# A delta-rule attention and soft-MoE kernel: block inverse, a wider join product, output products by batch row

## The chip, the cores and the metric

The kernel runs on one core of one Trainium2 chip. The metric is the device time of one execution in microseconds. A core has a matrix engine (TensorE, PE in the profile; PEld is its loading of weights), a vector engine (DVE), a scalar engine (ACT), a general engine (POOL) and a queue engine that issues transfers (SP). All data is fp32; the profile shows each fp32 matrix product as two instructions with a weight load each, and each transpose as one.

## The reference

```python
def _attn_ref(q, k, v, beta):                    # (4, 8, 768, 48)
    k_n = k / (np.linalg.norm(k, axis=-1, keepdims=True) + 1e-06)
    state = np.zeros((B, H, D, D))
    for t in range(S):
        y[:, :, t] = np.einsum('bhd,bhde->bhe', q[:, :, t], state)
        v_old = np.einsum('bhde,bhd->bhe', state, kt)
        state = state + bt * np.einsum('bhd,bhe->bhde', kt, vt - v_old)

def _moe_ref(x, phi, w1, w2):                    # x (3072, 384), phi (384, 32)
    logits = x @ phi                             # w1 (8, 384, 1024), w2 (8, 1024, 384)
    d = softmax(logits, axis=0); slot_input = (d.T @ x).reshape(8, 4, 384)
    for e in range(8):
        slot_out[e] = np.maximum(slot_input[e] @ w1[e], 0.0) @ w2[e]
    c = softmax(logits, axis=1)
    return c @ slot_out.reshape(32, 384)
```

The softmaxes are written out here in one word each. The attention output, with batch and time as rows and head and feature as columns, is x.

## The kernel before

The 768 time steps are cut into 12 chunks of 64, and the sequential update inside a chunk is replaced by a triangular system per head. There are 32 heads in all (4 batches of 8); a pair of heads shares the 128 partitions, and pairs are numbered j = 0 to 7, with i for one of two head groups and c for the half of the partitions.

For each chunk `prep` (line 653) loads k and q, turns them with eight 128x128 transposes each (`turn`, line 563), forms the Gram products k k and k q (`gram`, line 589), and copies the key part out of PSUM under row masks (`keys`, line 620, two ACT instructions per half: two of the three 32-column blocks at once, then the third). `pack` (line 675) adds the two 32-blocks on the diagonal of each head's 64x64 matrix for the inversion.

`invert` works on two chunks together. The matrices are spread (line 727) so that each partition holds two 16x16 blocks, and each block is inverted by columns on DVE: `scale` (line 767) multiplies all 16x16 entries by the weights, then `col(j)` for j = 0 to 14 makes a product (line 777) and a subtraction (line 781) over the rows below j. The results are turned back (lines 799 and 807) and copied into the layouts of the joins (`wide`, line 818).

`join` builds the 64x64 inverse from the 16x16 ones in two steps. From 16 to 32: the copies `far16`, the products `m16` (line 854: 16 per chunk, with weights of 128 rows and 64 columns, one head each, and 32 moving columns), copies `ev16` (line 862), the products `mo16` (line 872), and the correction at line 878. From 32 to 64: line 884 turns, line 895 copies, `mq` (906), `mo64` (917) and the correction at line 927.

`step(n)` then applies the chunk to the state: state times keys (959), the rest (966), the inverse times the rest (979), the copy of that result (1003), the update of the state (1017, 1026), and the output of the chunk from the state (989) and from inside the chunk (1041, copied at 1052). `route` turns the output (1077) and forms the logits (1102); `phase` keeps the running softmax over rows (1162 to 1191) with the slot products (1180).

The last stage starts when all chunks are through: line 1279 gathers the slot inputs, `first` multiplies with w1 (1304) and turns the hidden layer (1320), `combine` makes the softmax over slots (transposes 1120 and 1135, six each, and the DVE and ACT work at 1124 to 1137), `second` multiplies with w2 (1339) in two column halves of 192, line 1350 adds the expert parts, and line 1361 forms the output: for each stretch of 256 rows and each batch b two products with 32 rows of the combine weights against the 32 slots. DVE or ACT copies the result (1363), and SP sends it out (1365).

The order of all this is not the order of the program text. Every operation is recorded with an engine, a planned duration, the buffers it reads and writes and a key. A list scheduler (`Plan.schedule`) then plays the engines forward, picks per engine the ready operation with the longest remaining path plus its key, finds it room in SBUF (52,900 columns) and PSUM (eight banks), and the instructions are issued in that order, each engine in its own queue. Keys are shifted by the table `SHIFT`, one number for each kind of operation. The planner also models the supply of PE instructions in blocks (`FETCH`, `BESIDE`) and fills idle PE time in two stretches with products whose result is not used (line 480). Weight transfers start after chunk 6 (w1) and 10 (w2) and as soon as room is left (`WKEEP`, `W2KEEP`).

The lines that carry the change:

```python
            for j, i in pairs:                                       # m16, 16 products
                x = xi(i, j)
                mm(A(p16)[ha(i), 0, 32 * j:32 * j + 32], A(Gk[n])[:, 96 * x:96 * x + C],
                   A(z16)[:, 32 * x:32 * x + 32])
```

Of the kernel before, what the change touches and what calls it, by code (L numbers as in the profile page):

```python
# [16 lines left out]
SLACK = 4.53  # L17
HEAD = 40.0
SHIFT = {
# [45 lines left out]
class Tensor:  # L65
# [4 lines left out]
    BLOCK, AHEAD, FETCH, BESIDE = 256, 64, 3.8, 5.0  # L70
# [264 lines left out]
def kernel(  # L335
# [17 lines left out]
    nc = tc.nc  # L353
# [42 lines left out]
    def t_act(c):  # L396
        return 0.17 + 0.00071 * c
# [88 lines left out]
    W1AT, W2AT, W2KEEP = 6, 10, 8741  # L486
# [35 lines left out]
    for s_ in H2:  # L522
        for u in H2:
            def pick(s_=s_, u=u):
                for y in H2:
                    o = A(bsel)[0:32, P * (2 * s_ + u):P * (2 * s_ + u) + P].rearrange(
                        "p (c u s y i j) -> p u s y c i j", c=2, u=2, s=2, y=2, i=2)[:, u, s_, y]
                    x = ident()[0:32, 0:32].rearrange("p (y j i c) -> p y c i j", y=2, i=2, c=2)[:, y]
# [28 lines left out]
    def turn(src, n, w):  # L557
# [17 lines left out]
        pl.op("DVE" if dve else "ACT", t_dvp(1024) if dve else t_act(1024), ev, r=[ps], w=[(KQ[n], w)],  # L575
# [24 lines left out]
    def G3(n):  # L600
        return A(Gk[n]).rearrange("p (x b t) -> p x b t", b=3, t=32)

    def keys(n, j0, nj, ps, w):

        def ev(ys, i, lower):
            def go():
                i_ = A(ps).rearrange("p i (y j f) -> p i y j f", j=4, f=w)[..., 0:C].rearrange(
                    "p i y j (b t) -> p i y j b t", b=2)
                o = G3(n).rearrange("p (y i j) b t -> p i y j b t", y=2, i=2)
                i_, o, m = (i_[..., 1, :], o[..., 1, :], M1()) if lower else (i_, o[..., 0::2, :], M0())  # L610
                if i is None:
                    i_, o = i_[:, :, ys[0] - j0 // 4], o[:, :, ys[0]]
                elif len(ys) == 2:
                    i_, o = i_[:, i], o[:, i]
                else:
                    i_, o = i_[:, i, ys[0]], o[:, i, ys[0]]
                if i:
                    nc.vector.tensor_scalar(o, i_, m, None, op0=ALU.mult)
                else:
                    nc.scalar.activation(o, i_, ACT.Copy, scale=m)  # L620
            c = 512 if i is None and not lower else 256
            pl.op("DVE" if i else "ACT", t_dvp(c) if i else 0.61 if c == 512 else t_act(c), go, r=[(ps, i), cm0],
                  w=[(Gk[n], (lower, y, i)) for y in ys])
        for i in H2 if n == 1 else (None,):
            for y in range(j0 // 4, (j0 + nj) // 4):
                ev((y,), i, 0)
                if i is None:
                    ev((y,), i, 1)
            if i is not None:
                ev(H2, i, 1)  # L630
# [3 lines left out]
    def queries(n, j0, nj, ps, w):  # L634
# [8 lines left out]
        if j0 + nj == 8:  # L643
            qt = pl.buf(512)
            pl.op("ACT", 0.50, lambda: nc.scalar.activation(  # L645
# [9 lines left out]
    def prep(n):  # L655
# [16 lines left out]
        def pack():  # L672
            x = G3(n).rearrange("p x b t -> p b x t")
            o = A(Gd[n // 2]).rearrange("p (t s x) -> p s x t", s=2, t=32)[:, n % 2]
            (nc.vector if n == 1 else nc.gpsimd).tensor_tensor(o, x[:, 0], x[:, 1], op=ALU.add)  # L675
# [29 lines left out]
    def invert(gs):  # L705
        G = len(gs)
        head = gs[0] == 0
        if head:
            for n in H2:
                squares(n)  # L710
            for y, c in ((0, 0), (0, 1), (1, 0), (1, 1)):
                def turn_sq(y=y, c=c):
                    o = A(sqh)[ha(c ^ y)].rearrange("p (s y i j) -> p s y j i", s=2, y=2, i=2)[:, :, y]
                    x = A(sqn)[ha(c)].rearrange("p (s y j i) -> p s y j i", s=2, y=2, i=2)[:, :, y]
# [47 lines left out]

        def scale():
            for a in range(G):
                o = blk(lb, 0, 16, 0, 16)[:, 2 * a:2 * a + 2]
                m = A(gm)[:, 32 * a:32 * a + 32].rearrange("p (x t) -> p x t", x=2)
                V.tensor_tensor(o, o, m.unsqueeze(2).broadcast_to([P, 2, 16, 16]), op=ALU.mult)
        pl.op("DVE", (t_dv(512) + 0.08) * G, scale, r=[gm], w=[lb], port=True)
        pr = pl.buf(2 * G * 64)

        def col(j):
            m, w = j + 1, 15 - j

            def go():
                p = A(pr)[:, 0:2 * G * m * w].rearrange("p (x i k) -> p x i k", x=2 * G, k=m)
                sh = [P, 2 * G, w, m]
                V.tensor_tensor(p, blk(tt, j, j + 1, 0, m).broadcast_to(sh),  # L777
# [12 lines left out]
        for j in range(15):  # L790
            col(j)
# [606 lines left out]
```

## Time and profile before

| | us |
|---|---|
| median of 3 runs (lowest, highest) | 285.26 (282.96, 285.4) |
| the profiled execution, and its span | 285.92, 283.9 |
| PE products of line 589 / 563 / 1041 / 989 | 26.3 / 25.6 / 18.6 / 18.7 |
| PE unused products (line 480) | 23.6 |
| ACT copies of line 620 (47) | 25.6 |
| POOL `pack`, line 675 (11) | 14.2 |
| w1 and w2 transfers issued on SP | 164.0 to 259.8 |
| output transfers issued on SP | 262.8 to 280.9 |

The profile is of one execution. Busy times of engines overlap, so they do not add up to the span. The chain of waits is one path back from the last instruction: at each step to what released it, or to the instruction before it on the same engine. An engine's share of that chain says more about the end than its busy time.

### The profile page before, as it was taken

The page shows a single profiled execution, that of the slowest core. Times are in us where ns is not written, and L with a number is a line of the kernel's source. Part 1 is how long each engine was busy: PE and PEld are TensorE (multiplying, and loading weights), DVE is VectorE, ACT ScalarE, POOL GpSimd, SP SyncE. Part 2 cuts the span into 40 slices and gives each one's busy share as a digit, 9 for nine tenths or more (in the row PEclk, how much of TensorE's full clock was granted, in tenths as well). Part 3 has the DMA queues.
Part 4 walks back from the last instruction along what each step waited for, and adds up shares of the span by engine and source line. Part 5 has one row for each costly group of instructions (what it writes and reads, how often), then busy time and mean ns, then how long its engine had stood idle before and what let it go on. Part 6 is the DMA issues. An engine that isn't in the chain of part 4 may idle for free.

```text
span 283.9 us, 13766 instructions
## 1 busy us (share of the span) xinstructions
PE 253.4 (89%) x6038; PEld 211.2 (74%) x6038; DVE 203.6 (72%) x445; ACT 164.7 (58%) x350; POOL 99.0 (35%) x212
## 2 busy tenths in 40 slices
PE   8999998999987989797998998869997999999970
PEld 4777688898876978696986997768886896367860
DVE  2789988989688696789888796869971646941340
ACT  5556498678654698566778479671673452240330
POOL 8933476527730087404474027610330100000000
PEclk9999999999999999999999999989999999999995
DMA  8999982929436390066580994596997889999966
GB/s 99 142 137 145 137 90 41 135 43 139 59 50 68 68 106 3 2 82 93 99 75 2 125 236 97 163 228 218 330 373 265 246 249 322 328 301 329 289 216 223
DMA packets 105834, 45.11 MB, mean 159 GB/s; under 512 B 77008, under 2 KB 99568, under 8 KB 105776
## 3 DMA queue, kind: packets, MB, share of 16 engines
q1 hardware_dynamic: 105600, 44.05, 74.3%
q8 instruction: 47, 0.77, 1.2%
q10 hardware_dynamic: 48, 0.10, 0.3%
q0 software_dynamic: 128, 0.10, 0.2%
q14 instruction: 11, 0.09, 0.1%
HBM read 39.52 MB, written 4.72 MB: 156 GB/s over the span
## 4 chain that ended last, share of the span: by engine, by line
PE 65%; ACT 9%; DMA 7%; issue 6%; DVE 5%; SPq 3%; POOL 1%; ACTq 0%; DVEq 0%; POOLq 0%
DMA sb<-in_k_dram 7%; PE pb L589 6%; PE pb L563 6%; PE pb L989 5%; PE pb L959 5%; PE pb L979 5%; PE pb L480 4%; PE pb L872 4%; PE pb L1339 4%; PE pb L1304 4%; PE pb L1017 4%; PE pb L1041 4%; PE pb L854 3%; PE pb L917 2%; PE pb L1102 2%
## 5 line engine op out<-in xcount | busy, mean ns | idle before, releaser
L574 ACT ACTIVATE sb<-pb 128x1024 f32<-128x1024 f32 x23 | 23.5, 1025 | 17.5 <-PE pb L563 17.4
L620 ACT ACTIVATE sb<-pb,sb 128x256 f32<-128x256 f32 (+1 forms) x47 | 25.6, 574 | 7.1 <-PE pb L589 5.3
L777 DVE TENSOR_TENSOR sb<-sb 128x30 f32<-128x30 f32 (+7 forms) x90 | 27.0, 300 | 2.7
L589 PE MATMUL pb<-sb 48*64 48x64 f32 (+1 forms) x1024 | 26.3, 247 | 2.4 <-ACT sb L574 1.1
L589 PEld LDWEIGHTS pb<-sb 48*64 48x64 f32 x1024 | 22.3, 134 | 6.1 <-ACT sb L574 2.2
L563 PE MATMUL pb<-sb 128*128 128x128 f32 x192 | 25.6, 277 | 1.1 <-DMA sb<-in_k_dram 1.1
L781 DVE TENSOR_TENSOR sb<-sb 128x30 f32<-128x30 f32 (+7 forms) x90 | 23.7, 264 | 3.1
L675 POOL TENSOR_TENSOR sb<-sb 128x512 f32<-128x512 f32 x11 | 14.2, 1289 | 32.8 <-ACT sb L620 28.5
L480 PE MATMUL pb<-sb 128*128 128x512 f32 (+3 forms) x72 | 23.6, 456 | 1.1 <-DVE sb L449 1.1
L563 PEld LDWEIGHTS pb<-sb 128*128 128x128 f32 x192 | 20.9, 141 | 3.0 <-issue 1.4
L895 POOL COPY sb<-sb 32x128 f32<-32x128 f32 x48 | 13.7, 285 | 26.6 <-DVE sb L878 21.7
L1003 ACT COPY sb<-pb 64x768 f32<-64x768 f32 (+1 forms) x24 | 18.4, 765 | 6.1 <-PE pb L979 5.7
L1026 DVE TENSOR_TENSOR sb<-sb,pb 48x768 f32<-48x768 f32 x20 | 19.0, 952 | 3.7 <-PE pb L1017 3.3
L480 PEld LDWEIGHTS pb<-sb 128*128 128x128 f32 x72 | 13.0, 201 | 10.0 <-issue 7.8
L649 POOL TENSOR_SCALAR_AFFINE_SELECT sb<-sb 64x512 f32<-64x512 f32 x24 | 16.2, 676 | 11.1 <-ACT sb L645 6.9
L1041 PE MATMUL pb<-sb 128*64 128x96 f32 x384 | 18.6, 248 | 1.5 <-issue 1.5
L989 PE MATMUL pb<-sb 128*64 128x96 f32 x352 | 18.7, 260 | 0.0
L895 ACT COPY sb<-sb 32x128 f32<-32x128 f32 x48 | 14.2, 295 | 7.3 <-DVE sb L878 5.0
L1052 ACT ACTIVATE sb<-pb 128x768 f32<-128x768 f32 x11 | 8.9, 811 | 16.3 <-PE pb L1041 16.2
L1041 PEld LDWEIGHTS pb<-sb 128*64 128x64 f32 x384 | 16.6, 137 | 2.2 <-issue 1.9
L1017 PE MATMUL pb<-sb 128*48 128x96 f32 x352 | 16.9, 248 | 1.4 <-ACT sb L645 0.7
L884 DVE STREAM_TRANSPOSE sb<-sb 64x512 f32<-64x512 f32 x24 | 16.9, 705 | 0.6
(157 smaller groups left out, 544.9 us busy)
## 6 DMA issues: line engine op xcount, KB each, us to landing
sb<-in_moe_w_dram SPq DMA_DIRECT2D x48, 256.0 KB, 4.7
sb<-in_moe_w_dram SPq DMA_DIRECT2D x32, 384.0 KB, 6.6
sb<-in_k_dram SPq DMA_DIRECT2D x24, 192.0 KB, 5.5
sb<-in_v_dram SPq DMA_DIRECT2D x48, 96.0 KB, 4.4
sb<-in_q_dram SPq DMA_DIRECT2D x24, 192.0 KB, 6.1
out_dram<-sb SPq DMA_DIRECT2D x24, 192.0 KB, 2.5
sb<-in_beta_dram ACTq DMA_DIRECT2D x1, 96.0 KB, 4.9
sb<-in_moe_phi_dram POOLq DMA_DIRECT2D x2, 32.0 KB, 6.0
```

The costliest lines, as they stand in the source:

```text
L480: pl.filler = lambda b, w: mm(A(b)[:, 0, 0:w].rearrange("p (a f) -> p a f", f=min(w, P)), A(cone), A(cone)[:, 0:min(w, P)].unsqueeze(1).br ...
L563: nc.tensor.transpose(o[:, 128 * j:128 * j + 128], A(src)[:, 128 * j:128 * j + 128], ident())
L574: nc.scalar.activation(o, x, ACT.Copy)
L589: mm(A(ps)[ha(c ^ (j // 4)), i, w * (j - j0):w * (j - j0) + w], kq(n)[hd(i), j, c, 0:C], kq(n)[hd(i), j, c, lo:hi])
L620: nc.scalar.activation(o, i_, ACT.Copy, scale=m)
L777: V.tensor_tensor(p, blk(tt, j, j + 1, 0, m).broadcast_to(sh), blk(lb, j, j + 1, j + 1, 16).rearrange("p x a i -> p x i a").broadcast_to(s ...
L781: V.tensor_tensor(t, t, p, op=ALU.subtract)
L895: (nc.scalar.copy if by_act else nc.gpsimd.tensor_copy)(o[q:q + 32, :, c, i], zx()[64 * c + 32:64 * c + 64, y, i].rearrange("p (j t) -> p ...
L989: mm(ypart(j)[:, :, c], kq(n)[:, j, c, C:2 * C], S0()[:, j, c], start=b % 2 == 0 and c == 0)
L1017: mm(A(pS)[hd(i), j // 4, a:a + 2 * D], A(Kb[n])[:, 128 * j + 64 * i:128 * j + 64 * i + D], U0()[:, j // 4, i, j % 4])
L1026: nc.vector.tensor_tensor(o, o, x, op=ALU.add)
L1041: mm(ypart(j)[:, i], A(AT[n])[:, C * xi(i, j):C * xi(i, j) + C], U0()[:, j // 4, i, j % 4], start=n == 0 and b % 2 == 0 and i == 0)
```

## The change

Five things change, and a new order comes out of them.

1. `invert`: columns are only worked off inside the two 8x8 diagonal blocks of each 16x16 block (7 pairs instead of 15, on four blocks of 8 per partition), `scale` multiplies only those, and the 8x8 block below the diagonal is then formed by two products and two reductions. The POOL copy `place` goes; its place in the layout is taken by a different order of heads in the buffers, so that several access patterns change with it.

```diff
-        for j in range(15):
+        for j in range(7):
             col(j)
+        pl.op("DVE", 1.3, upper, r=[lb, tt], w=[pr], port=True)
+        pl.op("DVE", 1.15, lambda: V.tensor_reduce(
+            A(low), A(pr).rearrange("p (x j) -> p x j", j=8), axis=AX.X, op=ALU.add), r=[pr], w=[low])
+        pl.op("DVE", 1.3, lower, r=[low, tt], w=[pr], port=True)
+        pl.op("DVE", 1.3, below, r=[pr], w=[tt])
```

`upper` and `lower` each issue two DVE products of 512 elements per partition, `below` two reductions of 512 to 64.

2. `m16`: one product for both heads of a pair. The weights are 128 columns wide, the moving operand 64 columns; half of the result is not used.

```diff
-            for j, i in pairs:
-                x = xi(i, j)
-                mm(A(p16)[ha(i), 0, 32 * j:32 * j + 32], A(Gk[n])[:, 96 * x:96 * x + C],
-                   A(z16)[:, 32 * x:32 * x + 32])
-        o16 = pl.op("PE", **t_pe(16, 0.059, 32.0), fn=m16, r=[Gk[n], z16], w=[p16])
+            for j in range(8):
+                mm(A(p16)[:, 0, C * j:C * j + C], A(Gk[n])[:, 192 * j:192 * j + P], A(z16)[:, C * j:C * j + C])
+        o16 = pl.op("PE", **t_pe(8, 0.118, 64.0), fn=m16, r=[Gk[n], z16], w=[p16])
```

3. `keys`: the key blocks lie as (pair, head and block) instead of (head, block), and each of the three blocks is copied by an instruction of its own. For chunks 4 to 11 that is six copies of 256 elements instead of two of 512 and two of 256; for chunks 0, 2 and 3 three of 512.

4. The output products of the four batches are one operation, and the batches take turns; each batch has a PSUM bank of its own.

```diff
+                for par in H2:
+                    for b in range(B):
+                        rg = slice(32 * b, 32 * b + 32)
+                        mm(A(po[b])[:, 0, HD * par:HD * par + HD], A(cT)[rg, T0 + par:T0 + 256:2], A(so)[rg])
```

5. The plan: `combine` may start after the last chunk's product instead of after line 1279 (`combine(g, [chain[N - 1]])`); planned durations of ACT copies (`t_act`) go from 0.17 + 0.00071 c to 0.23 + 0.0007 c; `FETCH` 3.8 to 4.1 and `BESIDE` 5.0 to 6.0; `SLACK` 4.53 to 5.77; `W2KEEP` 8741 to 1000, `WKEEP` 4836 to 8236; and all of `SHIFT` is new. In the order that results, the w1 transfers come as 14 and 34 around the last v load instead of 6, 6 and 36 around the last two; the softmax transposes lie before and among the w1 products instead of just before and after them; and the output products of the first half take turns with the w2 products of the second.

More of the change, by code (lines that the diff above doesn't have):

```diff
@@ L574, in ev @@
                 nc.scalar.activation(o, x, ACT.Copy)
[L575 removed]
+        pl.op("DVE" if dve else "ACT", t_dvp(1024) if dve else 0.91, ev, r=[ps], w=[(KQ[n], w)],
               key=-30 if dve else 0)
@@ L617, in go @@
[L617 to L623, printed above, removed]
-        for i in H2 if n == 1 else (None,):
[L625 to L630, printed above, removed]
+                x = A(ps).rearrange("p i (j f) -> p j i f", f=w)[:, :, :, 32 * (b > 0):32 * (b > 0) + 32]
@@ new lines, in go @@
+                o, m = Gb(n, b)[:, j0:j0 + nj], M1() if b == 1 else M0()
+                if i is not None:
+                    o, x = o[:, :, i], x[:, :, i]
+                if i:
+                    nc.vector.tensor_scalar(o, x, m, None, op0=ALU.mult)
+                else:
+                    nc.scalar.activation(o, x, ACT.Copy, scale=m)
+            c = 32 * nj * (2 if i is None else 1)
+            pl.op("DVE" if i else "ACT", t_dvp(c) if i else t_act(c) + 0.03, go, r=[(ps, i), cm0], w=[(Gk[n], (b, j0, i))])
@@ L632 @@
+        for i in H2 if n == 1 else (None,):
+            for b in (0, 1, 2):
+                ev(i, b)
     APART = 4
@@ L761, in invert @@
         pl.op("DVE", W_, lambda: V.tensor_copy(dg(tt), sv(gm)), r=[gm], w=[tt])
+        d8 = lambda t, r0, r1, c0, c1: bass.AP(
+            tensor=A(t).tensor, offset=A(t).offset, ap=[list(A(t).ap[0]), [264, 4], [1, 264]])[
+            :, :, 0:256].rearrange("p x (r c) -> p x r c", c=32)[:, :, r0:r1, c0:c1]
         def scale():
[L764 to L767, printed above, removed]
@@ new lines, in invert, with upper, lower @@
+        lo8 = lambda x: A(low)[:, 64 * x:64 * x + 64].rearrange("p (i k) -> p i k", k=8)
+        sh8 = [P, 8, 8, 8]
+        def upper():
+            for x in H2:
+                V.tensor_tensor(p8(x), blk(lb, 0, 8, 8, 16)[:, x].rearrange("p j i -> p i j").unsqueeze(2).broadcast_to(sh8),
+                                blk(tt, 0, 8, 0, 8)[:, x].rearrange("p j k -> p k j").unsqueeze(1).broadcast_to(sh8), op=ALU.mult)
+        def lower():
+            for x in H2:
+                V.tensor_tensor(p8(x), blk(tt, 8, 16, 8, 16)[:, x].unsqueeze(2).broadcast_to(sh8),
+                                lo8(x).rearrange("p i k -> p k i").unsqueeze(1).broadcast_to(sh8), op=ALU.mult)
@@ new lines, in below @@
+        def below():
+            for x in H2:
+                V.tensor_reduce(blk(tt, 8, 16, 0, 8)[:, x], p8(x), axis=AX.X, op=ALU.add, negate=True)
+        pl.op("DVE", 0.14, lambda: V.transpose(A(nT), A(nrm)), r=[nrm], w=[nT])
+        for j in range(7):
+            col(j)
+        pl.op("DVE", 1.3, upper, r=[lb, tt], w=[pr], port=True)
+        pl.op("DVE", 1.15, lambda: V.tensor_reduce(
+            A(low), A(pr).rearrange("p (x j) -> p x j", j=8), axis=AX.X, op=ALU.add), r=[pr], w=[low])
@@ L1327 @@
     for g in range(NG):
-        combine(g, [ot3])
+        combine(g, [chain[N - 1]])
     for hc in H2:
```

112 lines of the change are left out of this document (49 added, 63 removed), and 45 rows, old and new, of the table SHIFT.

## The prediction

> **What bounds the kernel now.** I read the page's engine row first, then the chain of waits, then busy time by stretch, and last the groups that the change touches.
>
> ```profile
> PE 253.4 (89%) x6038; PEld 211.2 (74%) x6038; DVE 203.6 (72%) x445; ACT 164.7 (58%) x350; POOL 99.0 (35%) x212
> ...
> PE 65%; ACT 9%; DMA 7%; issue 6%; DVE 5%; SPq 3%; POOL 1%; ACTq 0%; DVEq 0%; POOLq 0%
> ```
>
> TensorE is busy nearly all the time and holds 65% of the chain. DVE is busy 72% but holds 5%: its work mostly lies beside TensorE's. "issue" is mostly TensorE stopping inside a product with nothing to wait for (at 72.7, 78.0, 87.1, 114.6, 170.8, 185.8, 212.9 and 216.8 us, 0.8 to 2.1 each). The page counts 47 instruction packets of 16 KB; in the trace they never start less than 4.04 us apart, so dense stretches of small products run out of instructions.
>
> ```profile
> 75.00:100.00 25.00, 22.75 (x632) 20.30 (x632) 19.28 (x48) 15.42 (x27) 5.18 (x18) 1.00 0.47 64
> 145.00:175.00 30.00, 27.49 (x776) 24.71 (x775) 23.79 (x54) 21.88 (x41) 10.01 (x24) 1.00 0.61 111
> 200.00:225.00 25.00, 21.87 (x662) 19.98 (x662) 15.82 (x21) 14.92 (x31) 5.91 (x14) 1.00 0.87 296
> ```
>
> The columns are length, then busy time of PE, PEld, DVE, ACT, POOL. In every stretch of the chunk loop PE is filled to 87 to 92%, so a product that gets longer can hide only in the rest. The groups concerned, then the weight loads of line 537 and the products of line 854 in time:
>
> ```profile
> L854 PE MATMUL pb<-sb 128*64 128x32 f32 x384 | 13.4, 223 | 0.0
> L1361 PE MATMUL pb<-sb 32*128 32x192 f32 x96 | 9.1, 342 | 0.5 <-DVE sb L1351 0.5
> L777 DVE TENSOR_TENSOR sb<-sb 128x30 f32<-128x30 f32 (+7 forms) x90 | 27.0, 300 | 2.7
> L781 DVE TENSOR_TENSOR sb<-sb 128x30 f32<-128x30 f32 (+7 forms) x90 | 23.7, 264 | 3.1
> ...
> 11.33 0.97 PEld L537 LDWEIGHTS pb<-sb 128*128 128x128 f32 x8
> ...
> 111.72 1.13 PE L854 MATMUL pb<-sb 128*64 128x32 f32 x32
> ```
>
> An fp32 product shows as two pieces. L854 is the first join product: 32 pieces whose weights are 64 columns wide, two column tiles side by side, in 1.05 to 1.13 us. L537 is the nearest row to what replaces it: weights 128 columns wide, 32 moving columns, eight pieces whose loads start 0.111 us apart.
>
> **First join product.** 32 pieces become 16 with 128-column weights and 64 moving columns. In L854 a pair of pieces starts every 0.058 us: 16 x 0.058 = 0.93. By L537's spacing the new one takes 16 x 0.111 = 1.78. So +0.85 us per chunk, 12 chunks, +10.2 us of TensorE. The lower bound is L854's own rate (0), if the width of the weights did not count; the upper is L537's second batch at 0.136 apart (+1.25, 15 us). I take 0.85, since L537's first batch has the same weight shape and fewer moving columns. The chain gives L854 4% of 283.9, 11.4 of its 13.4 us, so 0.85 of it is on the path: 8.7 us. Two things give back. 16 pieces fewer are 32 instructions (load and product) per chunk, 384 in all, 1.5 of the packets; at 4.05 each that is 6 us if every packet were awaited, but about 9 of some 38 in the loop are: -1.5. And TensorE's idle time takes in what lies just before it. It is 18 us between 54 and 240 (the same table over the whole loop), a tenth; gaps gather around the joins, so I take a sixth of 8.7: -1.5. Left: +5.7, bounds 0 and +10.
>
> Beside a rule: the Trainium skill (TensorEngine Tiling (Array Packing), Performance Considerations, Instruction Overhead) says that a product of 1 moving column takes as long as one of 60. By it alone half the pieces would take half the time; the trace's 0.111 for 32 moving columns under 128-column weights speaks against it, and this result is a rival below.
>
> **Array shape switches.** In the trace consecutive products of one array shape start 0.006 to 0.11 us apart across a change of line, and where the shape changes (128x64 to 64x64, 128x128 to 64x64) 0.15 to 0.20: about 0.1 each. The built program changes shape 142 times before and 167 after: 114 to 128 in the loop, 9 to 19 from the expert products on. +1.4 us in the loop, +1.0 in the end; bounds 0 and +4.
>
> **Inverse.** Lines 777 and 781 are 15 pairs per two chunks: 50.7 / 6 = 8.45 us, and 1 us of gaps. After: 7 pairs of 28 to 64 elements at about 0.23 (30 elements: 0.237 and 0.202; 56: 0.216 and 0.247), 3.2; two products of 512 at 0.69 twice (line 767), 2.8; reductions of 1024 and twice 512, from line 702 (768: 0.953) and line 1150 (256: 0.42), 1.2 + 1.4. Sum 8.6 with fewer gaps. The scaling falls from 512 elements (0.69) to 256 (about 0.45), and a 0.2 us POOL copy goes. Some 0.7 us of DVE per two chunks, 4 in all, hidden under TensorE: -0.3. Strided operands could make the new products slower (line 807 reads with a stride, 512 in 1.05): then +0.7 per pair of products, 8 us of DVE, of which by DVE's share of the chain 0.4 shows.
>
> **Key eviction.** For chunks 4 to 11 four ACT copies (two of 512 at 0.686, two of 256 at 0.476) become six of 256: +0.53 per chunk, 4.3 us of ACT. TensorE hides most; the chain holds this line around 99 to 101 and 138 us: +1.0 (0 to 4).
>
> **Head.** Before chunk 0 the new order runs the first join product ahead of the Gram product (1.16 us) that preceded it, so its 0.85 is covered there: 0 (-1 to +1).
>
> **Tail.** Products of line 1361 run two row groups at once: 48 pieces in 4.46 us on the chain. With four row groups in turn the trace's 0.162 us per round gives 12 x 0.162 = 2.0; upper bound the present 4.46.
>
> ```profile
> 261.32 4.46 PE pb L1361 x47
> 265.78 4.08 PE pb L1339 x96
> ...
> 271.41 0.93 PE pb L1361 x8
> ```
>
> The first half gains 2.4, provided the last w2 weights are there: before, they landed at 265.8, exactly when L1339 resumed. Their last issue (259.4) waits for room that line 1339's products free, and in the new order those products start earlier behind the expert products, so I let them come about 2 us sooner. The second half gains nothing: after the first copy the SP queue issues 12 output transfers 0.675 us apart, 8 us, whatever TensorE does. Six transposes of the softmax (0.55 us) leave the place ahead of line 1304; the other six stay inside. Together -3.0, with the switches -2.0.
>
> Here a rule would change the size: the Trainium skill (TensorE: Matmul & The Clock Gate, Measured speedup vs the span model) gives 3.07 for four row groups. By an estimate from it the half takes 48 x 0.162 / 3.07 = 2.5 and the gain is 1.9; no run so far shows four row groups.
>
> **Sum.** 5.7 + 1.4 - 0.3 + 1.0 + 0 - 2.0 = +5.8. The profiled execution took 285.9 (span 283.9), 0.7 above the median 285.26. In it TensorE's clock was halved from 189.4 to 192.8 us, after a stall of 2.1; the stretch of line 989 there took 2.62 instead of 1.47. I take off 1.2 for that and about 1 for waits that the recalibrated order (instruction supply 4.1 instead of 3.8, near the 4.05 seen) may avoid: 285.9 + 5.8 - 2.2 = 289.5.
>
> **The rivals.**
> *The longer product hides* (not slower, faster at the end). Point of decision: the waits of TensorE in the loop, 18 us between 54 and 240. If the new order puts the join products ahead of them and the instruction stops shrink by 6 rather than 1.5, the loop's 5.7 + 1.4 + 1.0 become about 1, and the tail's -2 to -3 and the clock's -1.2 remain: 285.9 + 1 - 0.3 - 2.5 - 1.2 = 282.9, and with 2 us saved by the order 281. For it: 9 stops of 0.8 to 2.1 us lie among just such products. Against: the chain charges L854 almost whole. If neither the width of the weights nor the moving columns counted, 16 pieces at L854's 0.029 would even take 0.47 less than now, 12 x 0.47 = 5.6: 275. That is what the Trainium skill's section on instruction overhead, named above, comes to. Chance of the first 0.25, of the second 0.03.
> *Half hides*: loop +4, tail and clock -3.2, order 0: 286.7. Chance 0.22.
> *The weights become the bound at the end.* In the new order the 23rd of 32 w2 tiles waits for the hidden-layer copies (before, the 26th did, 4.2 us). If the ten tiles after it follow at the 1.17 us of landings seen, the first half's 2.4 is lost beside the forecast's loop: 292. Chance 0.12, within the slower case.
>
> **How the numbers follow.** The forecast with its own range 286.5 to 292 has 0.38, the weights case 0.12. One per cent is about what a measurement of this kernel tells from no change: 282.4 to 288.1. Faster 0.28, same 0.22, slower 0.50. The range reaches from the hidden case with the better order, 280.5, to the weights case with 2 us of the unknown costs (strided inverse, key eviction), 294; the likeliest case's own range is 286.5 to 292.
>
> **What would show it.** Weight loads of the new join product 0.107 to 0.112 us apart, its group near 1.8 us each; PE busy near 258 with some 5800 pieces; inversion lines together near 8.6 us per two chunks; first-half output products near 2 us; output transfers still 0.67 apart from first copy to end; the start of line 1304's successor later than 240.6 by 4 to 7 us. I am wrong if the join's loads come at half that spacing, or if the loop reaches its last chunk no later than 227 us, where the last step's products start now.

## The result, and the profile after

The changed kernel takes 300.53 us (297.07 to 302.19, 4 executions), the kernel before 285.33 (282.96 to 286.94, 4) beside it: a ratio of 1.050, interval 1.037 to 1.063. It is slower by 15.2 us, where the forecast was 4.2 and the range ended at 294. The profiled execution took 297.07, its span is 295.4. Here and below a median is of all executions, and a ratio and its interval leave out those more than 1.5 per cent above the kernel's fastest.

The page of the changed kernel, its engine row, the clock row in 40 slices and the chain of waits:

```profile
PE 266.0 (90%) x5830; PEld 223.0 (76%) x5830; DVE 207.5 (70%) x391; ACT 167.3 (57%) x363; POOL 100.3 (34%) x206
...
PEclk9999755999999979999999999999799999999996
...
PE 56%; DVE 26%; issue 5%; ACT 3%; DVEq 0%; ACTq 0%
```

Three things are new. TensorE is busy 12.6 us longer with 208 pieces fewer. The clock row has three slices of 7, 5 and 5 early on. DVE's share of the chain has gone from 5 to 26%, though its busy time grew by only 3.9 us.

Busy time by stretch of the changed kernel (length, then PE, PEld, DVE, ACT and POOL; the last three numbers are granted clock, DMA share and GB/s): first two stretches of the head, then those that the prediction showed.

```profile
30.10:33.51 3.41, 0.89 (x9) 0.68 (x7) 3.38 (x5) 0.56 (x2) 0.39 (x1) 1.00 0.95 132
33.50:50.60 17.10, 17.10 (x182) 15.85 (x182) 8.70 (x15) 8.14 (x19) 7.23 (x14) 0.50 0.65 60
75.00:100.00 25.00, 24.52 (x584) 21.96 (x582) 20.12 (x40) 19.20 (x41) 12.73 (x27) 1.00 0.71 81
145.00:175.00 30.00, 28.47 (x692) 26.03 (x689) 23.89 (x42) 22.64 (x47) 13.71 (x28) 1.00 0.70 82
200.00:225.00 25.00, 22.44 (x489) 20.12 (x490) 22.04 (x37) 12.37 (x27) 5.04 (x10) 0.93 0.91 274
```

The same two stretches of the head in the kernel before:

```profile
30.10:33.51 3.41, 3.41 (x17) 2.08 (x16) 3.17 (x6) 0.55 (x1) 1.60 (x3) 1.00 1.25 141
33.50:50.60 17.10, 15.99 (x509) 14.22 (x509) 14.37 (x25) 15.41 (x34) 12.30 (x29) 1.00 0.66 78
```

In the changed kernel TensorE does 0.89 us of work between 30.1 and 33.5, and from 33.5 to 50.6 its clock is halved: it is busy all 17.1 us and gets 182 pieces done, against 509. The timeline ahead of that (start, duration, engine; idle time before the group and what ended it in brackets):

```profile
29.86 1.09 PE L564 MATMUL pb<-sb 128*128 128x128 f32 x8
...
30.50 1.26 DVE L799 TENSOR_REDUCE sb<-sb 128x64 f32<-128x512 f32 x2
31.80 1.91 DVE L815 STREAM_TRANSPOSE sb<-sb 128x512 f32<-128x512 f32 x2
...
32.93 0.40 ACT L860 COPY sb<-sb 64x256 f32<-64x256 f32 x1 [4.28 <-DVE sb L815]
...
33.47 2.76 PE L869 MATMUL pb<-sb 128*128 128x64 f32 x12 [2.52 <-ACT sb L860]
...
33.85 1.02 ACT L575 ACTIVATE sb<-pb 128x1024 f32<-128x1024 f32 x1
```

TensorE stands for 2.52 us in front of chunk 0's first join product (L869, 854 before): behind it in the queue lies the Gram product (L590, at 37.55), which needs nothing from the inversion. It couldn't have filled the gap by itself, though. Its operands are the transposes of 29.86, and their copy (L575, at 33.85) stands on ScalarE behind the copy for the join (L860), which waits 4.28 us for the inversion. So the order puts the inversion's followers first on two engines. In the kernel before, unused products of line 480 fill this place; the changed list gives the head 7,744 columns of those instead of 9,856.

Where the 12 us of the span arise is read from the starts of the state products (line 979, now 992) and of the w1 products (1304, now 1317):

| us | before | after | difference |
|---|---|---|---|
| state product of chunk 0 | 45.5 | 53.7 | +8.2 |
| state product of chunk 11 | 227.1 | 239.5 | +12.4 |
| first w1 product | 240.6 | 252.8 | +12.2 |
| output products, second half | 271.4 | 282.4 | +11.0 |

Two thirds of it is there at the first state product. Of the groups that the change touches:

```profile
L869 PE MATMUL pb<-sb 128*128 128x64 f32 x192 | 27.2, 302 | 2.6 <-ACT sb L860 2.5
...
L794 DVE TENSOR_TENSOR sb<-sb 128x512 f32<-128x512 f32 x12 | 13.0, 1127 | 0.1
...
L789 DVE TENSOR_TENSOR sb<-sb 128x512 f32<-128x512 f32 x12 | 12.3, 1066 | 0.1
...
L778 DVE TENSOR_TENSOR sb<-sb 128x28 f32<-128x28 f32 (+3 forms) x42 | 10.5, 249 | 1.5
...
L775 DVE TENSOR_TENSOR sb<-sb 128x28 f32<-128x28 f32 (+3 forms) x42 | 9.3, 220 | 1.3
...
L799 DVE TENSOR_REDUCE sb<-sb 128x64 f32<-128x512 f32 x12 | 7.6, 676 | 0.0
...
L804 DVE TENSOR_REDUCE sb<-sb 128x128 f32<-128x1024 f32 x6 | 7.3, 1219 | 0.2
```

The two block products of the inversion take 1.07 and 1.13 us an instruction. Lines 775 to 804 with the scaling (2.5) make 62.5 us, 10.4 per two chunks; before, scaling and columns were 9.1 (54.8 / 6).

### The profile page after: what moved, and what is told of

Same layout as the page of the kernel before. It is cut to its first block, busy times and chain, and to the rows that moved or that the text cites. A ratio compares the mean times of both kernels' runs of the same rounds, so it can differ in the third digit from the quotient of the medians.

```text
span 295.4 us, 13337 instructions
## 1 busy us (share of the span) xinstructions
PE 266.0 (90%) x5830; PEld 223.0 (76%) x5830; DVE 207.5 (70%) x391; ACT 167.3 (57%) x363; POOL 100.3 (34%) x206
## 4 chain that ended last, share of the span: by engine, by line
PE 56%; DVE 26%; issue 5%; ACT 3%; DVEq 0%; ACTq 0%
PE pb L869 8%; PE pb L1002 4%; PE pb L992 4%; DVE sb L789 4%; PE pb L886 4%; PE pb L1030 4%; PE pb L1352 4%; PE pb L1317 4%; PE pb L590 3%; DVE sb L794 3%; PE pb L564 3%; PE pb L972 3%; PE pb L1054 3%; DVE sb L1039 3%; DVE sb L778 2%
## 5 line engine op out<-in xcount | busy, mean ns | idle before, releaser
L575 ACT ACTIVATE sb<-pb 128x1024 f32<-128x1024 f32 x23 | 23.3, 1024 | 14.8 <-PE pb L564 14.7
L620 ACT ACTIVATE sb<-pb,sb 128x256 f32<-128x256 f32 (+1 forms) x60 | 27.7, 505 | 7.0 <-PE pb L590 5.5
L869 PE MATMUL pb<-sb 128*128 128x64 f32 x192 | 27.2, 302 | 2.6 <-ACT sb L860 2.5
L564 PE MATMUL pb<-sb 128*128 128x128 f32 x192 | 27.4, 290 | 1.9 <-POOL sb L669 0.6
L869 PEld LDWEIGHTS pb<-sb 128*128 128x128 f32 x192 | 25.6, 214 | 4.3 <-POOL sb L860 2.7
L590 PE MATMUL pb<-sb 48*64 48x128 f32 (+1 forms) x1024 | 27.1, 253 | 0.8 <-ACT sb L575 0.7
L590 PEld LDWEIGHTS pb<-sb 48*64 48x64 f32 x1024 | 22.8, 139 | 3.5 <-ACT sb L575 1.2
L1016 ACT COPY sb<-pb 64x768 f32<-64x768 f32 (+1 forms) x24 | 18.4, 767 | 12.4 <-PE pb L992 12.1
L564 PEld LDWEIGHTS pb<-sb 128*128 128x128 f32 x192 | 22.3, 148 | 3.7 <-issue 1.0
L992 PE MATMUL pb<-sb 64*64 64x48 f32 x768 | 15.4, 234 | 6.4 <-DVE sb L940 4.1
L992 PEld LDWEIGHTS pb<-sb 64*64 64x64 f32 x768 | 13.9, 149 | 8.1 <-DVE sb L940 4.0
L481 PE MATMUL pb<-sb 128*128 128x512 f32 (+3 forms) x56 | 18.4, 467 | 1.4 <-DVE sb L450 1.1
L644 POOL TENSOR_SCALAR_AFFINE_SELECT sb<-sb 64x512 f32<-64x512 f32 x24 | 18.1, 754 | 3.9 <-ACT sb L640 1.7
L972 PE MATMUL pb<-sb 128*64 128x96 f32 x352 | 17.5, 249 | 1.1 <-issue 0.6
L1054 PE MATMUL pb<-sb 128*64 128x96 f32 x384 | 18.4, 248 | 0.0
L1002 PE MATMUL pb<-sb 128*64 128x96 f32 x352 | 18.3, 261 | 0.0
```

Source lines behind the costliest of these rows:

```text
L564: nc.tensor.transpose(o[:, 128 * j:128 * j + 128], A(src)[:, 128 * j:128 * j + 128], ident())
L575: nc.scalar.activation(o, x, ACT.Copy)
L590: mm(A(ps)[ha(c ^ (j // 4)), i, w * (j - j0):w * (j - j0) + w], kq(n)[hd(i), j, c, 0:C], kq(n)[hd(i), j, c, lo:hi])
L620: nc.scalar.activation(o, x, ACT.Copy, scale=m)
L869: mm(A(p16)[:, 0, C * j:C * j + C], A(Gk[n])[:, 192 * j:192 * j + P], A(z16)[:, C * j:C * j + C])
L972: mm(A(pR)[ha(c ^ (j // 4)), j // 4, 2 * D * (j % 4):2 * D * (j % 4) + 2 * D], kq(n)[:, j, c, 0:C], S0()[:, j, c])
```

## The experiments

Three theories: (1) the wide join product costs what the forecast said, or more; (2) the halved clock in the head, which comes from the idle stretch ahead of chunk 0's join; (3) the long steps of the new inversion on DVE stand ahead of the state update. Each experiment ran beside the kernel before; the ratio to it is given with its interval where it decides.

**Width and clock.** Four kernels take the first two apart. a_half puts the 16 half-width products back, in the same list:

```diff
-            for j in range(8):
-                mm(A(p16)[:, 0, C * j:C * j + C], A(Gk[n])[:, 192 * j:192 * j + P], A(z16)[:, C * j:C * j + C])
+            for j, i in pairs:
+                z = C * j + 32 * i
+                mm(A(p16)[ha(i), 0, z:z + 32], A(Gk[n])[:, 192 * j + C * i:192 * j + C * i + C], A(z16)[:, z:z + 32])
```

> The changed kernel in its own order, with the first join product as before: 16 products per chunk, 64-column weights. If the width of the weights is the main cost (theory 1): 0.85 us less in each of 12 chunks, about 0.8 of it on the path, 8 us less than the changed kernel, and twice that for the two products that run at half clock: 290 to 292. If the halved TensorE clock at the start is the main cost (theory 2): the idle 2.5 us of TensorE before the first join product stays, the clock still halves near 33 us, and no more than 4 us come back: 296 to 298.

a_fill keeps the wide product and puts three unused products of 512 columns ahead of chunk 0's:

```diff
+            for _ in range(3 if n == 0 else 0):
+                pl.filler(p16, 512)
```

> The changed kernel with three unused products of 512 columns (2.6 us of TensorE) ahead of the first join product of chunk 0, where TensorE stood idle for 2.5 us; all else as it is. Theory 2 (the idle stretch halves the clock from 33.5 to 50.6 us): the clock stays whole, the first state product comes at 46 instead of 53.7 us, and 7 to 8 us come back: 292 to 293. Theory 1 (width of the weights): the clock stays whole too, but the chunk loop takes up what the head gains; 297 or more.

a_half_fill does both:

> Both: join product as before, and the three unused products. Theories 1 and 2 adding up: 8 + 7 us less than the changed kernel, 285 (284 to 287), as the kernel before. If the new inverse and order cost something of their own (theory 3: the new inverse's long DVE products stand ahead of the state update), it stays 3 us or more above the kernel before.

b_wide is the kernel before with the wide product alone. Its layout doesn't hold the two heads' weights side by side, so the second head of each pair is left out and the columns beside it are taken for weights; the work of every engine is that of a wide join.

```diff
-            for j, i in pairs:
-                x = xi(i, j)
-                mm(A(p16)[ha(i), 0, 32 * j:32 * j + 32], A(Gk[n])[:, 96 * x:96 * x + C],
-                   A(z16)[:, 32 * x:32 * x + 32])
+            for j in range(8):
+                x = xi(0, j)
+                mm(A(p16)[:, 0, C * j:C * j + C], A(Gk[n])[:, 96 * x:96 * x + P], A(z16)[:, 32 * x:32 * x + C])
```

> The kernel before, in its own order, with the first join product widened alone: 8 products per chunk with 128-column weights and 64 moving columns. It leaves out the second head of each pair (its result is not used rightly), the cost is that of the changed kernel's product. Theory 1: each group 1.75 us instead of 0.93, 0.85 of the 0.82 us times 12 on the path, less some hiding: 291 to 294. If the products hide in TensorE's waits: 285 to 287. If wide join products themselves make the clock halve (rival to theory 2): half-clock windows near 35 to 50 us although there is no idle stretch.

| | us | ratio to before (interval) | clock halved in the head |
|---|---|---|---|
| changed kernel | 300.5 | 1.050 (1.037 to 1.063) | 33.5 to 50.6 |
| a_half | 291.8 | 1.021 (1.012 to 1.029) | 34.1 to 47.8 |
| a_fill | 292.3 | 1.022 (1.013 to 1.031) | no |
| a_half_fill | 289.3 | 1.013 (1.005 to 1.021) | no |
| b_wide | 285.6 | 1.010 (1.004 to 1.014) | no |

In a_fill the head reads like that of the kernel before again; the columns are those above:

```profile
30.10:33.51 3.41, 3.41 (x17) 2.04 (x15) 2.97 (x5) 2.15 (x4) 1.06 (x2) 1.00 1.35 155
33.50:50.60 17.10, 16.36 (x438) 14.72 (x437) 13.53 (x28) 14.10 (x32) 12.22 (x28) 1.00 0.88 89
```

Work that computes nothing takes 8.2 us off: that is what the halved clock costs the changed kernel. With the clock whole the wide product costs 3.0 (a_fill less a_half_fill, whose intervals overlap), and in the order of before 1.2 to 4.1 (b_wide's interval of 284). With the clock halved it costs 8.7 (the changed kernel less a_half): its groups in the head then take 3.6 us each, and the half clock lasts 17.1 us instead of 13.7. The two costs don't simply add, and neither theory fits alone. a_half came out where theory 1 had put it, although its clock stays halved; b_wide came out below theory 1's time, a_half_fill above the sum of the two. With the half-width product the halved clock is worth only 2.4 us by medians (a_half less a_half_fill, overlapping again), though the profiles have chunk 0's state product 5.9 us earlier without it (44.3 against 50.2; 44.8 against 53.7 with the wide product). So theory 2 holds for the changed kernel, and theory 1 has the right sign at about half the forecast's size where the clock is whole.

**Does the new inversion cause the idle stretch, or slow the loop?** A first set lets the planner make a new list. b_inv is the kernel before with the new inversion alone, a_inv the changed kernel with the former one, ahc_inv the same on a kernel with half-width join, fillers and the combination's earlier place, and a_plan the changed kernel with the measured durations told to the planner:

```diff
-        o16 = pl.op("PE", **t_pe(8, 0.118, 64.0), fn=m16, r=[Gk[n], z16], w=[p16])
+        o16 = pl.op("PE", **t_pe(8, 0.224, 64.0), fn=m16, r=[Gk[n], z16], w=[p16])
...
-        pl.op("DVE", 1.3, upper, r=[lb, tt], w=[pr], port=True)
+        pl.op("DVE", 2.13, upper, r=[lb, tt], w=[pr], port=True)
```

> The kernel before with the new inversion alone (two 8-column blocks, the block below them by two products); join, order of the stages and output products as before. Theory 3: 10.4 us of VectorE per two chunks instead of 9.13 plus 1.2 of gaps, with long products standing ahead of the state update; the loop grows by 2 to 5 us and the kernel takes 286 to 289. Rival (what is left of the slowdown is the order of the changed kernel's list, not the inverse): within 1 us of before. My forecast's own reading (-0.3): 283 to 284.

> The changed kernel with the former inversion (15 pairs of operations, whole 16 columns) alone; join, layouts, key eviction, list order and output products as changed. If the late end of the new inversion is what leaves TensorE idle ahead of chunk 0's join and halves its clock, the clock stays whole there and the time falls by both costs, 8 for the clock and 3 for the inversion: 289 to 291. If the clock halves all the same (the order, not the inversion, starves TensorE there), only the inversion's 3 go: 296 to 298.

> The changed kernel with four things put back or added: half-width join, three fillers ahead of chunk 0, the last combination at its earlier place, and the former inversion. What stays of the change is the key eviction, the layouts, the output products by batch row and the recalibrated list. If the parts add up, the 287.6 of the same kernel with the new inversion falls by 3, to 284.5 or less, and with the output products' 2 us gained the list and the key eviction then cost some 2. If the inversion is not what the loop loses, it stays at 287 to 288.

> The changed kernel, with the planner told what the runs measured: 1.93 us for the wide join (it had 1.05), 2.13, 1.22, 2.25 and 1.35 for the four new steps of the inversion (it had 1.3, 1.15, 1.3, 1.3). Nothing computed differs. If the plan's wrong durations leave TensorE idle in the head and loop, it now puts fillers or other work there: no half clock around 33 us and 289 to 293. If the parts themselves cost the time: 298 to 301.

They took 287.1 (1.013, 1.008 to 1.018), 331.7, 322.5 and 315.4 us. The last three miss every theory: the state product of chunk 0 starts at 70.2, 70.8 and 65.0 us instead of 53.7. The table of key shifts goes with one set of planned durations; with others, even truer ones, the planner makes another list, here 15 to 35 us worse than the kernel that it was made from, and such runs compare lists, not inversions. b_inv has another list too, so its +1.3% is no price of the inversion either.

The next kernels therefore keep the list of TensorE, ScalarE, GpSimd and SyncE instruction by instruction and carry out the former 15 pairs (`pair(j)`, lines 777 and 781 of before) in the places of the new steps, with the planned times of those, seven in the column steps and two in each of the four behind: ai_same in the changed kernel, aif_same with a_fill's products, ahci_same in the kernel called ahf_comb below.

```diff
         def lower():
-            for x in H2:
-                V.tensor_tensor(p8(x), blk(tt, 8, 16, 8, 16)[:, x].unsqueeze(2).broadcast_to(sh8),
-                                lo8(x).rearrange("p i k -> p k i").unsqueeze(1).broadcast_to(sh8), op=ALU.mult)
+            for j in (11, 12):
+                pair(j)
```

> The changed kernel with the former inversion carried out in the places of the new one: seven pairs in the seven column steps, the other eight pairs two by two in the four steps behind. The list of every other engine is the changed kernel's, instruction by instruction. If the late end of the new inversion starves TensorE ahead of chunk 0's join and so halves its clock: the clock stays whole around 33 us and the time falls from 300.5 to 289 to 293. If the clock halves all the same (the list leaves too little ahead of the join, whatever the inversion): 297 to 300.

> The changed kernel with the former inversion in the places of the new one and three unused products of 512 columns ahead of chunk 0's join, so that the clock stays whole in the head: against a_fill (292.3) only the inversion differs. If the new inversion costs the loop 1 to 3 us: 289 to 291. If its VectorE time hides: 292 to 293. No half clock around 33 us, and no execution above 296.

> The same on top of the half-width join, the three fillers ahead of chunk 0 and the last combination at its earlier place (287.6 with the new inversion). Theory 3 (VectorE's longer steps stand ahead of the state update): the former inversion takes 1.2 us less VectorE per two chunks, and the time falls by 2 to 4, to 284 or less. If VectorE's work hides under TensorE: it stays at 287 to 288, and what is left of the slowdown belongs to the list and the key eviction.

| former inversion in the same list | us | the same with the new inversion | us |
|---|---|---|---|
| ai_same | 292.3 | changed kernel | 300.5 |
| aif_same | 292.9 | a_fill | 292.3 |
| ahci_same | 286.5 | ahf_comb | 287.6 |

Where the clock is whole in both (the last two rows), the new inversion comes out 0.6 us faster and 1.1 us slower by medians, and by the ratios to the kernel before (1.022 and 1.037, 1.011 and 1.005) 1.5 per cent faster and 0.6 slower. The pairs disagree in sign, and 286.5 lies between the two times expected. So nothing bears out the 2 to 4 us of theory 3: as far as these runs can tell, 1.3 us more DVE per two chunks hides, whatever DVE's share of the chain. A cost of 1 us is not ruled out.

ai_same seems to say that the new inversion halves the clock. Its profile says otherwise. The stretches of ai_same:

```profile
30.10:33.51 3.41, 1.25 (x12) 1.04 (x11) 3.21 (x9) 0.95 (x3) 0.39 (x1) 1.00 0.81 130
33.50:50.60 17.10, 16.06 (x418) 14.40 (x419) 13.68 (x26) 14.14 (x31) 11.83 (x27) 1.00 0.75 80
```

and the join's row in its timeline:

```profile
33.08 1.97 PE L863 MATMUL pb<-sb 128*128 128x64 f32 x16 [2.16 <-ACT sb L854]
```

TensorE still stands 2.16 us in the same place, 0.36 less. The half-clock stretches of one execution begin at whole multiples of 3.413 us from each other (33.5, 105.2 and 211.0 in the changed kernel: 21 steps and 31 more). In twelve profiles (both kernels, a_half, a_fill, a_half_fill, b_wide, b_key, b_out, ahf_comb, ahf_rows, ai_same and ahci_same) there are 18 such stretches before the last microseconds: 14 follow a step with 0.59 to 1.71 us of TensorE work, four a step with 2.65 to 2.79, all of these at 243 to 247 us. The work of one step does not decide alone: steps with 1.70 and 1.72 in a_half and 1.76 in ai_same are followed by the whole clock, and in aif_same one with 2.27 by the half. In ai_same the grid fell so that the idle time was split over two steps, and the lower held 1.76. And one of its four executions took 299.3 us at a mean clock of 0.947, where the others had 0.974 to 0.989 and 289.8 to 293.5. a_fill1 tests that: the new inversion, with a single product of 256 columns in the gap.

```diff
+            for _ in range(1 if n == 0 else 0):
+                pl.filler(p16, 256)
```

> The changed kernel with one unused product of 256 columns (two pieces, about 0.45 us) ahead of chunk 0's join: new inversion, and about 2.1 us of idle time left, as with the former inversion. If the length of the idle time and its place against the 3.41-us steps decide: some executions at 289 to 293 with a mean clock of 0.97 or more, others at 296 to 300 with 0.95, the share set by chance. If the new inversion as such halves the clock: all at 297 to 301.

Six executions: 291.5, 291.8 and 292.3 us at a mean clock of 0.971 to 0.976, and 298.3, 299.3 and 303.9 at 0.941 to 0.947. Its idle time was 2.1 us. One of the latter is the profiled one:

```profile
30.10:33.51 3.41, 1.31 (x11) 0.94 (x9) 3.38 (x5) 0.54 (x2) 0.39 (x1) 1.00 1.12 136
33.50:50.60 17.10, 17.10 (x198) 15.85 (x202) 8.71 (x15) 8.14 (x19) 7.22 (x14) 0.52 0.59 63
```

The same program falls into two times, half and half, and which it is goes with the clock. So the new inversion as such does not halve it. That the place of the gap on the grid decides is how the two profiles read: here the whole gap lies in the step from 30.7 to 34.1 us, in ai_same it is split. One execution of each was profiled, so this is not shown. With 2.52 us of idle time all four executions of the changed kernel had a mean clock of 0.939 to 0.950.

**How the block products are laid out.** ahf_rows is a_half_fill with the products of lines 789 and 794 written and read with the contiguous index innermost; the reductions then read with a stride.

```diff
-        p8 = lambda x: A(pr)[:, 512 * x:512 * x + 512].rearrange("p (i k j) -> p i k j", i=8, k=8)
+        p8 = lambda x: A(pr)[:, 512 * x:512 * x + 512].rearrange("p (i j k) -> p i j k", i=8, k=8)
...
-                V.tensor_reduce(blk(tt, 8, 16, 0, 8)[:, x], p8(x), axis=AX.X, op=ALU.add, negate=True)
+                V.tensor_reduce(blk(tt, 8, 16, 0, 8)[:, x], p8(x).rearrange("p i j k -> p i k j"), axis=AX.X,
+                                op=ALU.add, negate=True)
```

> The changed kernel with the half-width join and the fillers ahead of chunk 0 (289.3 us), and with the two new block products of the inversion written and read so that their innermost index is contiguous; the reductions behind them read with a stride instead. Same arithmetic, same planned order. Theory 3 (the inverse's block products are long because of how their operands are laid out, and stand ahead of the state update): the products fall from 1.13 and 1.07 us each towards the 0.69 of a contiguous 512-column product, VectorE has some 1.6 us less per two chunks, and the time falls to 286 to 287.5. If layout is not what costs, the products stay above 1 us, or the reductions take what the products lose, and the time stays at 289 to 290.

Its groups (the products, then the two reductions):

```profile
L799 DVE TENSOR_REDUCE sb<-sb 128x64 f32<-128x512 f32 x12 | 12.5, 1085 | 0.0
L805 DVE TENSOR_REDUCE sb<-sb 128x128 f32<-128x1024 f32 x6 | 12.3, 2042 | 0.2
...
L794 DVE TENSOR_TENSOR sb<-sb 128x512 f32<-128x512 f32 x12 | 7.7, 686 | 0.1
L789 DVE TENSOR_TENSOR sb<-sb 128x512 f32<-128x512 f32 x12 | 7.7, 680 | 0.1
```

The products fall to 0.68 us, the price of a contiguous one, and the reductions rise from 0.68 and 1.22 to 1.09 and 2.04: 10 us saved, 10 lost. The time is 289.6 (ratio 1.015, 1.005 to 1.024) against 289.3. Here the stride costs the same in either place.

**The other parts.** ahf_comb is a_half_fill with the last combination behind the slot inputs again, as before:

```diff
-        combine(g, [chain[N - 1]])
+        combine(g, [ot3])
```

> The changed kernel with the half-width join and the fillers ahead of chunk 0 (289.3 us), with the last combination put back to its earlier place in the list, so that the order at the end changes. If the half clock around 243 us, behind the last chunk, comes from the order there and costs: no half-clock stretch there, and 1 to 2 us less (287.5 to 288.5). If the end is set by other work: 289 to 290.

It took 287.6 (1.011, 1.002 to 1.020): 1.8 less than a_half_fill by the medians, which the intervals can't separate. The edit also brings unused products of line 481 back into the end of the list. In the profiles the stretch between the last two state products is 11.5 us instead of 14.1; a half-clock step at 219.6 lies in the latter, so how much is the clock's stays open.

b_key is the kernel before with its 512-column key copies cut into two, in its own order:

```diff
-                    nc.scalar.activation(o, i_, ACT.Copy, scale=m)
+                    for b in H2:
+                        nc.scalar.activation(o[..., b, :], i_[..., b, :], ACT.Copy, scale=m)
```

> The kernel before, in its own order, with each 512-column key copy of chunks 4 to 11 cut into two of 256 alone, as the changed kernel has them. The forecast's term: 4.3 us more ScalarE, of which 1.0 shows: 285 to 286. If it hides altogether: within 0.5 of before. If the copies sit on TensorE's path as the chain's rows near 99 and 138 us suggest: 287 or more.

The edit cuts all 22 copies of 512 columns, those of chunks 0, 2 and 3 too, so it asks more of ScalarE than the change does: 32.6 us for the key copies, their times added up (69 instructions), against 30.3 in the changed kernel (60) and 27.0 before (47). It took 286.3 beside 284.8, ratio 1.003 (0.998 to 1.008): no difference that these runs can tell, and at most 2.4 us.

b_out is the kernel before with the output products by batch row in turn alone:

> The kernel before with the output products by batch row in turn alone. The forecast's term: the products of the first half go from 4.46 to about 2.6 us (the changed kernel showed 2.6) and the time falls by 1.9, to 282 to 282.5. Rival: the end is set by the output transfers, so an earlier first half only makes them wait, and the time stays within 0.7 of before.

The edit is part 4 of the change as its diff shows it. It took 281.96 (280.61 to 282.56) beside 284.3, ratio 0.989 (0.982 to 0.997): less than either kernel of this case. The chain of waits in b_out (start, duration, line 1361 being the output products, now 16 pieces at a time between the w2 products):

```profile
257.03 0.79 PE pb L1339 x16
257.82 0.87 PE pb L1361 x16
258.69 1.44 PE pb L1339 x32
260.13 0.87 PE pb L1361 x16
261.00 1.44 PE pb L1339 x32
262.43 0.87 PE pb L1361 x16
263.30 1.48 PE pb L1339 x32
```

The 48 pieces of the first half take 2.6 us instead of 4.46. From the first w1 product to the end the two profiles take 41.7 us (b_out) and 43.3 (before); the other 3.5 us between their spans lie ahead of that, where the two lists are the same, so the edit accounts for 1.6 of the 5.1.

**The sum.** From 300.5, by medians: the halved clock in the head 8.2, the width 3.0, the place of the combination 1.8, the inversion nothing measurable. That leads to 287.6 beside 284.3. The 11.2 of the first two are theirs together; taken the other way round they are 8.7 for the width and 2.4 for the clock. Only the step from the changed kernel has intervals that lie apart; 3.0 and 1.8 are differences of medians. The 3.2 that remain contain the gain of the output products, 2.4 by medians, so the new list, the changes of array shape and the key copies cost some 5.6 together, a figure that inherits the doubt of all these terms. Which of them has how much was not taken apart, beyond b_key's bound.

## Why the prediction was wrong

The sign was right, the size was not: +4.2 forecast, +15.2 measured. Step by step:

- *Head, 0 (-1 to +1).* This is the step that failed: it priced the new order by the product that runs first (0.85 us, "covered there") and didn't ask what TensorE would have to do until the inversion was through. The order puts the join, which waits for the inversion, ahead of the Gram product on TensorE, puts the join's copy ahead of that of the Gram product's operands on ScalarE, and takes unused products away. The idle 2.52 us lead to 17.1 us at half clock. Measured: +8.2 with the wide product. The prediction had seen the mechanism in the profile of before, a halved clock from 189.4 to 192.8 after a stall of 2.1 us, and used it only to take 1.2 off.
- *First join product, +5.7 (0 to +10).* Mechanism right: loads start 0.111 us apart, a group takes 1.93 us in the chain against 1.05, +0.85 a chunk as forecast, and full-rate groups lie on the chain. Of the 10.2 us that it adds to TensorE 3.0 show by medians, 1.2 to 4.1 in b_wide; the sum had let 5.7 show. The share of the path in that sum was misread, as the row behind this list shows. The rule of the Trainium skill (TensorEngine Tiling (Array Packing), Performance Considerations, Instruction Overhead), by which half the pieces would take half the time, is not borne out here: 1.93 against 1.05 us.
- *Inversion, -0.3.* DVE's part was mis-sized: 0.7 us less per two chunks was forecast, 1.3 more came (10.4 against 9.1; with the gaps, which shrank from 1.2 to 0.55, 0.65 more), because the block products cost 1.07 and 1.13 with strided operands instead of 0.69. That was the bound named there, and so was its small effect: the time showed no difference that these runs can tell.
- *Key eviction, +1.0.* Within b_key's interval (-0.7 to +2.4 us), which doesn't tell it from nothing. ScalarE's part was 3.3 us instead of 4.3: chunks 0, 2 and 3 each save a copy, which the term left out.
- *Array shape switches, +1.4 and +1.0.* Not tried alone; they lie in the rest of 5.6.
- *Tail.* The first half takes 2.6 us instead of the 2.0 of the forecast. The Trainium skill's 3.07 (TensorE: Matmul & The Clock Gate, Measured speedup vs the span model) gave an estimate of 2.5, which the trace bears out better. The gain of the output products alone is 1.0 to 5.1 us by b_out's interval, 2.4 by medians and 1.6 in the profiles; the forecast had 2.4 for them. The last rival, that the w2 weights become the bound, did not come about: the changed kernel's chain holds no DMA.
- *The recalibrated order, -1.* Wrong in sign: the gap in the head is the list's (2.16 us of it stay with the former inversion) and the main loss; what else the list costs lies in the 5.6.

The share of the path: the chain by line, from the page of the kernel before.

```profile
DMA sb<-in_k_dram 7%; PE pb L589 6%; PE pb L563 6%; PE pb L989 5%; PE pb L959 5%; PE pb L979 5%; PE pb L480 4%; PE pb L872 4%; PE pb L1339 4%; PE pb L1304 4%; PE pb L1017 4%; PE pb L1041 4%; PE pb L854 3%; PE pb L917 2%; PE pb L1102 2%
```

L854 has 3%, not 4: seven of its twelve groups, 7.2 us of 13.4 and not 11.4. With 0.54 in place of 0.85 the same working gives 5.5 - 1.5 - 0.9 = 3.1, nearer to the 3.0 than these runs can test.

Of the signs named, PE busy came to 266 instead of 258, with 5,830 pieces as said: 17 us of it ran at half clock, and a_fill, with the clock whole in the head, has 260.8 with 2.6 of added products in it. The w1 products came 12.2 us late instead of 4 to 7. None of the rivals had a new wait in the head, which is where one was missing. Without the halved clock the kernel (a_fill, 292.3) lies inside the range, but not by the forecast's sum: the join costs less than its term, and the 5.6 by medians stand against +2.4 for switches, key copies and order.

## What to carry to other kernels

When an edit comes with a new order, walk the new order on the bounding engine, and on the engine that prepares its operands, and ask at each instruction that waits what stands behind it and what fills the time; here a gap of 2.5 us cost 8.2, because the clock halved behind it. A list tuned for given durations is part of the kernel: compare a part only with the list held, instruction by instruction, or the lists are compared. A share of the chain that grows, like DVE's here, tells whom the engine waits for, not what shortening that work would bring.

## What the runs showed of the hardware

- The clock stays halved though TensorE is busy all the time: 17.1 of 17.1 us in five steps of 3.413 us, 13.7 in four with the half-width join. Later in the changed kernel's loop it came back after one step. The Trainium skill (TensorE: Matmul & The Clock Gate, Part 1: The HAM clock gate) has a free-running window of 3413 ns, and the grid here agrees; it has the clock back after one busy window, which these 17.1 us, by busy time in the profile, do not bear out. What tells these stretches apart from the others was not tried.
- Behind an idle time of 2.1 us, shorter than a step, the clock halved in 3 of 6 executions, behind one of 2.52 in 4 of 4; for those that were not profiled this is judged by their mean clock. The times of a_fill1 lie in two groups, 6 to 12 us apart.
- A DVE product of 512 fp32 elements takes 1.07 to 1.13 us in the layout with a strided operand and 0.68 without (ahf_rows); a reduction of 512 takes 1.09 instead of 0.68. Moving the stride from one to the other changed nothing in the sum.
